# Order of the two transforms in a couple of ticks, and which banks they use

## The chip, the cores and the metric

The kernel runs on one core of a Trainium2 chip. The metric is the device time of one execution in microseconds; the figure for a kernel is the median of its runs. Engines are named as the profile names them: PE (TensorE matmuls), PEld (TensorE weight loads), DVE (VectorE), ACT (ScalarE), POOL (GpSimd) and SP (SyncE, which here only issues DMAs).

## The reference

`x` is (8, 5696, 128), eight batches. First a causal convolution along the sequence with the filter `h`, written as a product of spectra of the doubled length; then a spectral mix of the lowest 64 modes of that result, and a residual with one dense layer:

```python
Yf = rfft(x, n=2*S, axis=1) * rfft(h, n=2*S, axis=0)[None]
a  = irfft(Yf, n=2*S, axis=1)[:, :S]                  # (8, 5696, 128)
X  = rfft(a, axis=1)[:, :64]                          # 64 modes, complex
Y  = X times (w_r + i w_i), one 128x128 matrix per mode
u  = a + irfft(Y, n=S, axis=1)
out = u + relu(u @ w_ch)
```

## The kernel before

The sequence is cut as 5696 = 89 x 64, and every Fourier transform is made of matmuls with constant matrices in fp16. The batches go two at a time: four passes, `g_` = 0 to 3. A pass has a first transform (`a_tile`, 32 of them: a slice of `Xin` times `F1`, evacuated to `As`), then 26 ticks. In a tick `t` below 23, up to four of the 90 values of `k` are worked on, and four kinds of work follow one another:

- `second(g_, t)`, the second transform: 16 matmuls of `M` and `As` (64 rows in use, 128 columns), two accumulated per value of `k` and batch, into a slot of two PSUM banks, one per batch. The profile shows them as `ps<-As,M`. Sixteen is one tick, thirty-two is two ticks one behind the other.
- `products(g_, t, slot)`, the product with the filter's spectrum `Hs` on DVE, into one of three buffers `U` (L651). As a rule ACT first copies the slot from PSUM to a small fp16 buffer `Xs` (`copied`, one of two buffers), and DVE multiplies from there. In a tick called *straight* (`t % 4 == 3` in the passes after the first) there is no copy: DVE reads the slot in PSUM itself (the rows `U<-ps,Hs` of 2048 columns).
- With a lag of two ticks, `ps<-U,Wc`: four matmuls of 512 columns that turn `U` back along one axis, two per batch, into one of three PSUM banks (`ZBANK`) in turn. ACT evacuates each to `Zs` or `Zt`, and SP writes that to memory.
- With a lag of three ticks, `ps<-G,Zs`: sixteen short matmuls that gather the 64 modes in a bank of their own.

Each engine works through its own list in order; a recorder (`R.add`) follows which instruction reads and writes what, and adds semaphore waits between engines.

In the passes after the first, `twin(g_, t)` is true for odd `t`: the second transforms of `t` and `t + 1` are then issued together, and tick `t + 1` issues none. I call the two ticks a couple: (1,2), (3,4), ... (21,22). Those that start with a straight tick are (3,4), (7,8), (11,12), (15,16) and (19,20): five in a pass, fifteen in the three passes. In them the second tick is copied by ACT as a rule is.

The slot is one of `XSLOT = [0, 2]`, that is banks 0 and 1, or banks 2 and 3. A second transform that writes a slot must wait until ACT's copy, or DVE's straight product, has read what stood there.

In the same ticks DVE also places the next pass's input (`x_place`, L365, eight copies `Xin<-Xt` per pass), which POOL loads (`x_load`, two DMAs each, `Xt<-in_x_dram`, issued in tick `t` once the product of tick `t` is done). The last of the eight is loaded in tick 16 and placed at the top of tick 22; the next pass's first transform waits for all of them. A pass ends with the first transforms of the next one. After the fourth pass come the mix of the modes and the output stage (`u_tile`, `o_tile`).

Of the kernel before, what the change touches and what calls it, by code (L numbers as in the profile page):

```python
# [123 lines left out]
def bass_long_conv_fft__then__afno_spectral_mix_kernel(nc, x, h, moe_w_r, moe_w_i, moe_w_ch, out):  # L124
# [160 lines left out]
    def ap(t, row, p0, n, off, dims):  # L285
        return bass.AP(t, p0 * row + off, [[row, n]] + [list(d) for d in dims])
# [5 lines left out]
    def pv(bank, off, dims, p0=0, n=P):  # L292
        return bass.AP(ps, p0 * 4096 + bank * 512 + off, [[4096, n]] + [list(d) for d in dims])
# [5 lines left out]
    def bank(i):  # L299
        return ("bank", i)  # L300
# [3 lines left out]
    def evac(dst, src, reads, writes, scale=None, eng=None, after=()):  # L304
        e = eng
        if e is None:
            turn[0] ^= 1
            e = "scalar" if turn[0] else "vector"
        if e == "scalar":
            if scale is None:  # L310
                R.add(e, lambda h_: h_.copy(dst, src), reads, writes, after=after)  # L311
            else:
                R.add(e, lambda h_: h_.activation(dst, src, COPY, scale=scale), reads, writes, after=after)  # L313
        elif scale is None:
            R.add(e, lambda h_: h_.tensor_copy(dst, src), reads, writes, after=after)  # L315
        else:
            R.add(e, lambda h_: h_.tensor_scalar_mul(dst, src, scale), reads, writes, after=after)  # L317
# [4 lines left out]
    def mm(o, l, r, st, sp, reads, writes):  # L322
        R.add("tensor", lambda h_: h_.matmul(o, l, r, start=st, stop=sp), reads, writes)  # L323
# [11 lines left out]
    def turns(name, items):  # L335
        i = ring2.get(name, 0)
        ring2[name] = i + 1
        return items[i % len(items)]
# [25 lines left out]
    def x_place(i, src, toks):  # L364
        R.add("vector", lambda e: e.tensor_copy(bass.AP(x_sb, i * XN * XS, [[XW, NQ], [XS, XN], [1, D]]),  # L365
                                                src),
              list(toks) + XZ, [("xin", i)])
# [51 lines left out]
    def mtok(k):  # L419
        t = [("m", k // KP)]  # L420
        if k % KP == KP - 1 and k < NK - 1:
            t.append(("m", k // KP + 1))
        return t

    W1, W2, WI = wc_sb[:, 0:P], wc_sb[:, P:2 * P], wi_sb[:, :]
    XSLOT = [0, 2]
# [14 lines left out]
    for j in range(16):  # L441
        t = turns("h", [0, 2, 4])
# [36 lines left out]
    def xtok(n):  # L479
        return [("xt", n, p_) for p_ in range(2)]  # L480

    def x_room(g_, i):
        if g_ > 1:
            return x_st[i]
        return x_h[i] if i < NXH else x_st[i - NXH]
# [97 lines left out]
    def with_h_at(g_, t):  # L583
        return g_ == 0 and t + LH < NT
# [3 lines left out]
    def copied(g_, t, sl):  # L588
        n = len(ticks[t])
        e = onchip[(g_, t)] = turns("e", list(range(NXS)))  # L590
        evac(bass.AP(x_s[e], 0, [[1024, P], [512, 2], [1, n * D]]), pv(sl, 0, [[512, 2], [1, n * D]]), [bank(sl), bank(sl + 1)],
             [("xs", e)], eng="scalar")
        return e

    def twin(g_, t):
        return g_ > 0 and t % 2 == 1

    def straight(g_, t):
        return g_ > 0 and t % 4 == 3

    def slot_of(g_, t):
        if t == 0:
            return ZSLOT
        if g_ == 0:
            return XSLOT[(t + 1) % 2 if not with_h_at(g_, t) else 0]
        return XSLOT[((t - 1) // 4 + t) % 2]

    def second(g_, t, d0=0, d1=D, bs=(0, 1)):
        sl = slot_of(g_, t)
        rd = AST if d1 == D else [("as", j) for j in range(d1 // 4)]  # L610
        for i, k in enumerate(ticks[t]):
            for r in range(2):
                for b in bs:
                    col = k * 3 * J + (J if r == 0 else 0) + b * J
                    mm(pv(sl + b, i * D + d0, [[1, d1 - d0]]),
                       ap(m_sb, MW, J * b, J, col, [[1, P]]),
                       ap(a_sb, AW, J * b, J, (2 * k + r) * D + d0, [[1, d1 - d0]]), r == 0, r == 1,
                       rd + mtok(k), [bank(sl + b)])

    def first_u(b, s_, row, tok, d0, d1):  # L620
        n = len(ticks[0])
        R.add("vector", lambda e: e.tensor_tensor(  # L622
            bass.AP(u_s[0], b * 512 + d0, [[2048, P], [1024, 2], [D, n], [1, d1 - d0]]),
            bass.AP(s_[0], s_[1] + d0, [[row, P], [0, 2], [D, n], [1, d1 - d0]]),
            bass.AP(h_sb, d0, [[2 * HW, P], [HW, 2], [D, n], [1, d1 - d0]]), MULT),
              [tok, ("h", 0, 0), ("h", 0, 1, 0), ("h", 0, 1, J)], [("u", 0)])
# [36 lines left out]
    def tick(g_, t):  # L663
        if g_ + 1 < NP:
            for i in range(2 * XC):
                if t == XPLACE[g_ > 0][i]:
                    x_place(i, bass.AP(x_room(g_ + 1, i), 0, [[XB, NQ], [D, XN], [1, D]]), xtok(i))
        with_h = with_h_at(g_, t)
        if t < NT:
            of_two = t > 0 and twin(g_, t - 1)  # L670
            if not of_two:
                if t:
                    second(g_, t)
                if t == 1:
                    d_ = DA if g_ else DF
                    second(g_, 0, d_, D, (0,))
                    first_u(0, (ps, slot_of(g_, 0) * 512), 4096, bank(slot_of(g_, 0)), d_, D)
            products(g_, t, slot_of(g_, t))
            if twin(g_, t):
                second(g_, t + 1)  # L680
                if straight(g_, t):
                    copied(g_, t + 1, slot_of(g_, t + 1))
        drain = list(border[t]) if t in border and g_ + 1 < NP else []
        if drain and t >= NT:
            j, sl, e = drain.pop(0)
            a_tile(j, [sl], e)
        if g_ + 1 < NP:
            i = t // 2 - 1 if t % 2 == 0 else -1
            if g_ == 0:
                i = XLATE.index(t) + NXH if t in XLATE else -1  # L690
            if 0 <= i < 2 * XC:
                x_load(g_ + 1, i, x_room(g_ + 1, i), xtok(i), [("u", t % NU)] + AST)
        if LC <= t < NT + LC:
            s_ = t - LC
            n = len(ticks[s_])
            i, zi = s_ % NU, zroom(g_, s_)
            zb = [turns("z", ZBANK) for b in range(2)]
            for b in range(2):
                for r in range(2):
                    mm(pv(zb[b], 0, [[1, n * D]]), (W1, W2)[r], u_s[i][:, r * 1024 + b * 512:r * 1024 + b * 512 + n * D],  # L700
                       r == 0, r == 1, [("u", i), ("wc",)], [bank(zb[b])])
                evac(bass.AP(z_s[zi], b * D, [[1024, P], [2 * D, n], [1, D]]),
                     pv(zb[b], 0, [[D, n], [1, D]]), [bank(zb[b])], [("zs", zi, b)], eng="scalar",
                     after=once(("zx", zi, b), Z_OLD) if zi >= NZ else ())
            zo = (g_ * NK + KT * s_) * P * 256
            dma("sync", bass.AP(zs, zo, [[256, P], [P * 256, n], [1, 256]]),
                bass.AP(z_s[zi], 0, [[1024, P], [256, n], [1, 256]]), "z",
                [("zs", zi, 0), ("zs", zi, 1)], [("zd", g_, s_)])
            if drain and t >= NT:
                j, sl, e = drain.pop(0)  # L710
                a_tile(j, [sl], e)
        if LM <= t < NT + LM:
            s_ = t - LM
            zi = zroom(g_, s_)
            for i, k in sorted(enumerate(ticks[s_]), key=lambda q: (s_ > 0 or q[1] != 1, q)):
                for b in range(2):
                    if k % 2:
                        o, off, n, sl = pv(MB, b * P, [[1, P]]), (k + 1) // 2 * P, P, (k + 1) // 2
                    else:
                        ms, off = even[k]  # L720
                        n, sl = 2 * len(ms), 0
                        dims = [[M, 2]] if len(ms) == 1 else [[ms[1] - ms[0], 2], [M, 2]]
                        o = pv(MB, b * P + ms[0], dims)
                    mm(o, z_s[zi][:, i * 256 + b * P:i * 256 + b * P + P], g_sb[:, off:off + n],
                       k == 1 and b == 0, k == NK - 1 and b == 1, [("g", sl // GP), ("zs", zi, b)], [bank(MB)])
        if drain and t < NT + LM - 1:
            j, sl, e = drain.pop(0)
            a_tile(j, [sl], e)
        if with_h:
            filter_tick(t + LH, [2, 3])  # L730
# [230 lines left out]
```

## Time and profile before

| | |
|---|---|
| median of 3 runs | 378.37 us (377.17, 378.37, 379.49) |
| profiled execution, its own time | 377.96 us |
| its span on the core | 376.1 us |
| granted TensorE clock, mean | 0.992 |
| first pass, with the filter's own transform between its ticks | about 46 to 96 us |
| ticks of the second, third and fourth pass | about 108 to 143, 162 to 198, 217 to 255 us |
| mix and output stage | from about 256 us to the end |

The profile is one execution. Times in it are microseconds from the span's start. A row of its timeline gives the start, the time until the end of the last instruction merged into the row, the engine, the line, the operation, the output and the inputs, the shape, and the count; a bracket tells how long the engine sat idle before it, and what released it. On ACT and DVE the recorded end of an instruction lies somewhat behind the start of the next one, so the pace of an engine is read from start to start. All matmuls are issued from one helper line (L323), all plain ACT copies from another (L311), so groups go by the tiles' names.

### The profile page before, as it was taken

The numbers are of one execution on the slowest core, as the hardware profiler recorded it, in microseconds if no ns is written. First come the engines' busy times: TensorE is split into PE (matmuls) and PEld (weight loads), VectorE is DVE, ScalarE is ACT, GpSimd is POOL, SyncE is SP. The second block draws the span as 40 slices with busy tenths as digits, with TensorE's granted clock in tenths as the row PEclk, the third lists the DMA queues.
The fourth block names the chain that finished last, engine by engine and source line by source line (L and its number), as shares of the span: only waits on it lengthen the run. The fifth ranks groups of instructions, "written<-read, shape, count | busy, mean of one in ns | idle before, by whom it ended". The sixth has DMA issues, their size and how long they took to land.

```text
span 376.1 us, 12494 instructions
## 1 busy us (share of the span) xinstructions
PE 357.8 (95%) x5370; PEld 278.1 (74%) x5370; DVE 294.3 (78%) x335; ACT 315.7 (84%) x497; POOL 75.0 (20%) x117
## 2 busy tenths in 40 slices
PE   7979999999999999999998999999999999999994
PEld 7978866666866666856666856668889988888873
DVE  3548889978998999989998988883447767756666
ACT  8458899998999997989997999996557677688885
POOL 8703011200643220742310301124000000000000
PEclk9998999999999999999999999999999999999998
DMA  7999979979799997999995989999999999999878
GB/s 145 206 283 367 244 178 252 210 212 269 85 154 198 251 247 214 96 145 214 257 256 163 99 301 365 372 356 378 358 410 399 417 410 409 410 405 379 316 303 324
DMA packets 87048, 103.94 MB, mean 276 GB/s; under 512 B 22730, under 2 KB 72522, under 8 KB 83438
## 3 DMA queue, kind: packets, MB, share of 16 engines
q1 hardware_dynamic: 64610, 81.33, 61.1%
q0 software_dynamic: 22384, 21.83, 35.4%
q8 instruction: 42, 0.69, 0.7%
q14 instruction: 12, 0.10, 0.1%
HBM read 70.61 MB, written 51.12 MB: 324 GB/s over the span
## 4 chain that ended last, share of the span: by engine, by line
PE 67%; ACT 11%; DMA 10%; DVE 5%; issue 3%; POOL 3%; SPq 0%; DVEq 0%; POOLq 0%
PE ps L323 67%; ACT As L313 7%; DMA Hs<-Hs 4%; DMA Xr<-in_x_dram 4%; DVE As L317 2%; DMA Xt<-in_x_dram 2%; POOL Xr L320 2%; ACT Zs L311 1%; ACT R L893 1%; POOL Hin L320 1%; DVE Xin L365 1%; ACT Xs L311 1%; DVE U L622 1%; DVE Hs L315 1%; ACT Zt L311 1%
## 5 line engine op out<-in xcount | busy, mean ns | idle before, releaser
L651 DVE TENSOR_TENSOR U<-Xs,Hs 128x2048 f16<-128x2048 f16 (+1 forms) x73 | 86.6, 1192 | 13.9 <-ACT Xs L311 11.4
L323 PE MATMUL ps<-U,Wc 128*128 128x512 f16 (+1 forms) x368 | 94.1, 376 | 1.4 <-DVE U L622 1.4
L311 ACT CAST Xs<-ps 128x1024 f16<-128x1024 f32 (+1 forms) x77 | 74.7, 978 | 7.3 <-PE ps L323 4.2
L311 ACT CAST Zs<-ps 128x512 f16<-128x512 f32 (+1 forms) x132 | 69.2, 595 | 1.9 <-PE ps L323 1.9
L894 DVE TENSOR_TENSOR O<-ps,R 128x512 f32<-128x512 f32 x81 | 52.3, 684 | 20.7 <-ACT R L893 11.8
L317 DVE TENSOR_SCALAR As<-ps 128x720 f16<-128x720 f32 (+1 forms) x67 | 55.8, 881 | 6.7 <-PE ps L323 5.2
L893 ACT ACTIVATE R<-ps 128x512 f32<-128x512 f32 (+1 forms) x92 | 50.5, 592 | 9.0 <-PE ps L323 8.9
L323 PE MATMUL ps<-F,Xin 128*128 128x180 f16 x512 | 53.5, 254 | 4.4 <-DVE Xin L365 2.9
L323 PEld LDWEIGHTS ps<-F,Xin 128*128 128x128 f16 x512 | 45.8, 155 | 11.7 <-DVE As L317 3.3
L323 PE MATMUL ps<-As,M 64*128 64x128 f16 (+3 forms) x1504 | 52.3, 214 | 2.1 <-ACT As L313 1.3
L313 ACT ACTIVATE As<-ps 128x720 f16<-128x720 f32 (+1 forms) x65 | 46.2, 769 | 8.4 <-PE ps L323 7.8
L323 PE MATMUL ps<-WI,UT 128*128 128x256 f16 x360 | 51.0, 278 | 0.5 <-ACT UT L311 0.4
L323 PEld LDWEIGHTS ps<-U,Wc 128*128 128x128 f16 x368 | 28.7, 97 | 30.3 <-ACT Zs L311 3.7
L311 ACT CAST UT<-ps 128x712 f16<-128x712 f32 x46 | 34.5, 752 | 17.8 <-PE ps L323 16.8
L323 PEld LDWEIGHTS ps<-As,M 64*128 64x128 f16 x1504 | 42.2, 94 | 8.5 <-ACT As L313 1.8
L323 PEld LDWEIGHTS ps<-WI,UT 128*128 128x128 f16 x360 | 39.0, 152 | 3.4 <-issue 1.8
L323 PE MATMUL ps<-IBs,C 128*128 128x356 f16 x128 | 39.2, 314 | 0.2
L320 POOL DMA_DIRECT2D Xt<-in_x_dram x40 | 21.5, 541 | 78.7 <-PE ps L323 78.2
L323 PEld LDWEIGHTS ps<-G,Zs 128*128 128x128 f16 x512 | 26.1, 96 | 14.5 <-ACT Zs L311 2.0
L651 DVE TENSOR_TENSOR U<-ps,Hs 128x2048 f16<-128x2048 f32 x15 | 34.2, 2283 | 0.0
L323 PE MATMUL ps<-G,Zs 128*128 128x128 f16 (+2 forms) x512 | 32.2, 192 | 0.1
L311 ACT CAST Zt<-ps 128x512 f16<-128x512 f32 x52 | 28.5, 622 | 0.4 <-PE ps L323 0.4
(74 smaller groups left out, 480.0 us busy)
## 6 DMA issues: line engine op xcount, KB each, us to landing
out_dram<-O SPq DMA_DIRECT2D x39, 512.0 KB, 8.7
zscr<-Zs SPq DMA_DIRECT2D x62, 256.0 KB, 6.1
zscr<-Zt SPq DMA_DIRECT2D x26, 256.0 KB, 6.3
Xt<-in_x_dram POOLq DMA_DIRECT2D x20, 320.0 KB, 6.9
W<-wscr SPq DMA_DIRECT2D x4, 1024.0 KB, 7.2
ZT0a<-zscr SPq DMA_DIRECT2D x4, 1024.0 KB, 9.9
M<-cM POOLq DMA_DIRECT2D x5, 720.0 KB, 17.6
ZT1a<-zscr SPq DMA_DIRECT2D x3, 1024.0 KB, 10.6
```

Source lines behind the costliest of these rows:

```text
L311: R.add(e, lambda h_: h_.copy(dst, src), reads, writes, after=after)
L313: R.add(e, lambda h_: h_.activation(dst, src, COPY, scale=scale), reads, writes, after=after)
L315: R.add(e, lambda h_: h_.tensor_copy(dst, src), reads, writes, after=after)
L317: R.add(e, lambda h_: h_.tensor_scalar_mul(dst, src, scale), reads, writes, after=after)
L320: R.add(eng, lambda h_: h_.dma_start(dst, src), reads, writes, ring=ring, after=after)
L323: R.add("tensor", lambda h_: h_.matmul(o, l, r, start=st, stop=sp), reads, writes)
L365: R.add("vector", lambda e: e.tensor_copy(bass.AP(x_sb, i * XN * XS, [[XW, NQ], [XS, XN], [1, D]]), src), list(toks) + XZ, [("xin", i)])
L622: R.add("vector", lambda e: e.tensor_tensor(bass.AP(u_s[0], b * 512 + d0, [[2048, P], [1024, 2], [D, n], [1, d1 - d0]]), bass.AP(s_[0], s_ ...
L651: R.add("vector", lambda e: e.tensor_tensor(uv, src, hv, MULT), bk + [("h", t, 0), ("h", t, 1, 0), ("h", t, 1, J)], [("u", i)])
L893: R.add("scalar", lambda e: e.activation(rv, src_r, RELU), bk, [("r", i % NR)], after=once(("r", i % NR), G_ALL + XTT + [("y", 0), ("y", 1 ...
L894: R.add("vector", lambda e: e.tensor_tensor(ov, src_u, rv, ADD), bk + [("r", i % NR)], [key + (h_,)], after=once(key, old))
```

## The change

In a couple that starts with a straight tick, the second transform of `t + 1` is issued ahead of that of `t`. DVE's straight product and ACT's copy of `t + 1` are issued in the same places as before. The slots go by `t % 4`: ticks with remainder 0 and 1 take banks 0 and 1, those with 2 and 3 take banks 2 and 3.

```diff
     def slot_of(g_, t):
...
-        return XSLOT[((t - 1) // 4 + t) % 2]
+        return XSLOT[t % 4 // 2]
...
         if t < NT:
             of_two = t > 0 and twin(g_, t - 1)
             if not of_two:
+                if straight(g_, t):
+                    second(g_, t + 1)
                 if t:
                     second(g_, t)
...
             products(g_, t, slot_of(g_, t))
-            if twin(g_, t):
+            if straight(g_, t):
+                copied(g_, t + 1, slot_of(g_, t + 1))
+            elif twin(g_, t):
                 second(g_, t + 1)
-                if straight(g_, t):
-                    copied(g_, t + 1, slot_of(g_, t + 1))
```

In the order in which PE writes them, the slots before were, from tick 1 on, 2, 0, 2, 0 for ticks 1 to 4, then 0, 2, 0, 2 for 5 to 8, and so on by turns; now they are 0, 2, and then always 0, 2 again, where the copied tick of a straight couple comes first and takes banks 0 and 1, and the straight tick takes banks 2 and 3. So the lists of all five engines keep their length and their sequence of kinds. What differs in the waits is this: in each of the fifteen straight couples ACT's copy waits for a matmul 16 places earlier in PE's list than before, and DVE's straight product for one 16 places later.

## Prediction

> **What bounds the kernel now.** I read the page first, then the windows of the passes that the change touches, then the chain of waits, and last the timeline of one straight couple on PE, ACT and DVE. The page says that PE is at work almost all the time, and that the chain that ended last runs mostly through it:
>
> ```profile
> span 376.1 us, 12494 instructions
> PE 357.8 (95%) x5370; PEld 278.1 (74%) x5370; DVE 294.3 (78%) x335; ACT 315.7 (84%) x497; POOL 75.0 (20%) x117
> PE 67%; ACT 11%; DMA 10%; DVE 5%; issue 3%; POOL 3%; SPq 0%; DVEq 0%; POOLq 0%
> ```
>
> The windows give, for a stretch, its length and then the busy time of PE, PEld, DVE, ACT and POOL, the granted clock, the DMA share and GB/s. The first row is the ticks of the third pass, the second those of the fourth, the third a part of the output stage. Under them is a piece of the chain (start, length, engine):
>
> ```profile
> 162.50:198.00 35.50, 35.46 (x548) 22.61 (x549) 33.69 (x28) 34.42 (x56) 8.74 (x16) 1.00 1.06 224
> 217.30:252.00 34.70, 34.64 (x544) 22.18 (x545) 28.92 (x21) 33.63 (x54) 5.37 (x3) 1.00 1.02 347
> 263.00:314.00 51.00, 50.90 (x777) 45.39 (x774) 32.63 (x47) 33.64 (x56) 0.00 (x0) 1.00 1.01 399
> 162.54 27.27 PE ps L323 x430
> ```
>
> PE is the pace: 35.46 of 35.50 us, at full clock, and the chain stays on it for 27.27 us. ACT and DVE are close behind (34.42 and 33.69). So a matmul moved within PE's list is worth nothing by itself. The change can pay only through a wait inside PE's dense stretch, and a recorded matmul hides a short one. I look for it by comparing a straight couple with a plain one. Ticks 7 and 8 of the third pass are the couple at 170.55, ticks 9 and 10 the one at 174.11:
>
> ```profile
> 170.55 1.07 PE L323 MATMUL ps<-As,M 64*128 64x128 f16 x32
> 171.55 1.04 PE L323 MATMUL ps<-U,Wc 128*128 128x512 f16 x4
> 172.75 1.07 PE L323 MATMUL ps<-U,Wc 128*128 128x512 f16 x4
> 173.66 0.52 PE L323 MATMUL ps<-G,Zs 128*128 128x2 f16 x8
> 174.11 1.07 PE L323 MATMUL ps<-As,M 64*128 64x128 f16 x32
> 175.11 1.04 PE L323 MATMUL ps<-U,Wc 128*128 128x512 f16 x4
> 176.31 1.02 PE L323 MATMUL ps<-U,Wc 128*128 128x512 f16 x4
> 177.18 0.49 PE L323 MATMUL ps<-G,Zt 128*128 128x2 f16 x8
> 177.59 1.07 PE L323 MATMUL ps<-As,M 64*128 64x128 f16 x32
> ```
>
> The work is the same. The straight couple takes 174.11 - 170.55 = 3.56 us, the plain one 177.59 - 174.11 = 3.48. The 0.08 lies in two places: the second group of `U,Wc` (1.07 against 1.02) and the short matmuls behind it (0.52 against 0.49). Who holds them is seen on ACT and on PEld:
>
> ```profile
> 171.06 0.63 ACT L311 CAST Zs<-ps 128x512 f16<-128x512 f32 x1
> 171.66 1.01 ACT L311 CAST Xs<-ps 128x1024 f16<-128x1024 f32 x1
> 172.57 0.59 ACT L311 CAST Zs<-ps 128x512 f16<-128x512 f32 x1
> 172.57 1.08 ACT L311 CAST Zs<-ps 128x512 f16<-128x512 f32 x2
> 173.22 0.11 PEld L323 LDWEIGHTS ps<-U,Wc 128*128 128x128 f16 x2 [0.36 <-ACT Zs L311]
> 175.76 1.07 ACT L311 CAST Zt<-ps 128x512 f16<-128x512 f32 x2
> 176.72 1.03 ACT L311 CAST Xs<-ps 128x1024 f16<-128x1024 f32 x1
> ```
>
> There are three banks for the results of `U,Wc`. The third matmul at 172.75 (the second batch) writes the bank that ACT's evacuation at 172.57 empties. That one ends at 172.57 + 0.59 = 173.16, and the weight load goes at 173.22, released by it. The second evacuation of that pair ends at 172.57 + 1.08 = 173.65, when the short matmuls that read it begin (173.66). So in a straight couple PE runs into ACT, by 0.08 us.
>
> And ACT was late because of the copy in front: two evacuations take 176.72 - 175.76 = 0.96 from start to start, 0.48 each. ACT could have begun the copy at 171.06 + 0.48 = 171.54, but it began at 171.66, as the 32 matmuls ended (170.55 + 1.07 = 171.62). It waited 0.12 us for the second half of the couple.
>
> **The change part by part.**
>
> *ACT's copy.* In the changed order the copied tick is complete after the first 16 matmuls, half of 1.07: about 170.55 + 0.54 = 171.09. ACT is ready only at 171.54, so the copy starts there, 0.12 earlier. The two evacuations behind it move with it, since their matmuls (171.55 to 172.59) leave them room: 173.16 becomes 173.04, and with the 0.06 from there to the weight load 173.10. Without a stall, the third matmul is due at 172.75 + 2 x 0.217 = 173.18 (four of them take 177.18 - 176.31 = 0.87 from start to start in the plain couple). The bank is free in time by 0.08. The short matmuls, due 0.05 earlier at 173.61, find their data at 173.53. Both stalls go: 0.08 per straight couple, five a pass. PE is then late next on itself, at 3.48 per couple as in plain ones; ACT had 35.50 - 34.42 = 1.08 idle in the window of a pass, and keeps it.
>
> *DVE's straight product.* It now waits for all 32 matmuls, half a couple (0.54) more. DVE's rows, of ticks 6 and 7, and then of ticks 1 to 3 of the second pass with ACT's copy beside them:
>
> ```profile
> 170.81 1.23 DVE L651 TENSOR_TENSOR U<-Xs,Hs 128x2048 f16<-128x2048 f16 x1 [0.73 <-ACT Xs L311]
> 171.95 2.28 DVE L651 TENSOR_TENSOR U<-ps,Hs 128x2048 f16<-128x2048 f32 x1
> 107.82 2.35 DVE L651 TENSOR_TENSOR U<-Xs,Hs 128x2048 f16<-128x2048 f16 x2
> 110.09 2.28 DVE L651 TENSOR_TENSOR U<-ps,Hs 128x2048 f16<-128x2048 f32 x1
> 110.04 1.01 ACT L311 CAST Xs<-ps 128x1024 f16<-128x1024 f32 x1 [0.36 <-PE ps L323]
> ```
>
> Before the straight product DVE is busy with the product in front of it, so it comes at 171.95, when the couple has been complete since 171.62: 0.33 to spare, and the longer wait costs nothing. In the first straight couple of a pass the margin is small. There the copy, which in the old order waits for the same 32 matmuls, goes at 110.04, and the product at 110.09: 0.05 to spare. The Trainium skill, "Perfetto Trace Analysis", section "Tensor Engine Instruction (MATMUL, LD_WEIGHTS)", says that a matmul's end in a profile is estimated from its size and not observed. By that rule the 0.33 could be wrong, while the start of the copy at 110.04 stands, being an observed start on ACT; the trace agrees in that the copies start 0.04 behind the modelled ends (171.66 against 171.62). So I take this part at 0, between 0 and a delay of 0.54.
>
> *Slots.* Each write of a slot follows the reader of two transforms earlier, as before: the first of a straight couple follows a copy, the second a copy, and in the next couple the first follows the copy and the second the straight product. The straight product ends at 171.95 + 2.28 = 174.23; the transform that overwrites its slot is the second half of the couple at 174.11, that is 174.65. It has 0.42 to spare, 0.34 when PE comes 0.08 earlier. Ticks 1 and 2 swap slots behind the first transforms, but tick 1 waits for all of those in either order. I take 0.
>
> *What arrives at the end of a pass.* The gain must pass the placing of the next input, where PE waits:
>
> ```profile
> 144.31 0.85 PE L323 MATMUL ps<-F,Xin 128*128 128x180 f16 x8 [0.33 <-DVE Xin L365]
> 199.10 0.85 PE L323 MATMUL ps<-F,Xin 128*128 128x180 f16 x8 [0.54 <-DVE Xin L365]
> 138.49 2.28 DVE L651 TENSOR_TENSOR U<-ps,Hs 128x2048 f16<-128x2048 f32 x1
> 140.69 0.68 DVE L365 COPY Xin<-Xt 89x2048 f16<-89x2048 f16 x1
> 141.28 2.36 DVE L651 TENSOR_TENSOR U<-Xs,Hs 128x2048 f16<-128x2048 f16 x2
> 143.57 0.68 DVE L365 COPY Xin<-Xt 89x2048 f16<-89x2048 f16 x1
> 188.23 1.22 DVE L651 TENSOR_TENSOR U<-Xs,Hs 128x2048 f16<-128x2048 f16 x1
> 190.98 7.35 DMA Xt<-in_x_dram
> 198.35 0.69 DVE L365 COPY Xin<-Xt 89x2048 f16<-89x2048 f16 x1
> 190.98 0.93 POOL L320 DMA_DIRECT2D Xt<-in_x_dram  x1 [0.48 <-issue]
> 191.11 0.68 DVE L365 COPY Xin<-Xt 89x2048 f16<-89x2048 f16 x1
> 135.39 1.04 POOL L320 DMA_DIRECT2D Xt<-in_x_dram  x2 [2.29 <-PE ps L323]
> ```
>
> In the second pass DVE runs without a break from the straight product of tick 19 (138.49) to the last `Xin` (143.57). So the gains of the four earlier straight couples arrive, 4 x 0.08 = 0.32. In the third pass the last `Xin` at 198.35 waits for its load, which took 7.35 us from 190.98 (198.33). That load is issued behind the product of tick 16 (188.23), so it moves with the three couples before: 3 x 0.08 = 0.24. In the fourth pass no input is placed: 5 x 0.08 = 0.40. The output stage is PE's own (50.90 of 51.00) and moves as a whole. The sum is 0.32 + 0.24 + 0.40 = 0.96 us.
>
> A rule of the Trainium skill bears on the third pass: "SBUF — State Buffer", section "Who interferes with whom", says that a DVE copy can take the port pair shared with GpSimd for its whole length and so hold up the writing of DMA descriptors. The rows agree: the issue at 190.98 that met the copy at 191.11 took 0.93, where two in the second pass took 1.04 together. By that rule the term would be 0.24 if the copy and the issue still meet, as I expect since both hang on the same products, and up to 0.41 more (0.93 less half of 1.04) if they don't.
>
> **The sum.** The profiled execution took 377.96 us, 1.86 more than its span; less 0.96 it is 377.00. It lies 0.41 below the median of the three runs, so for a median I say 378.37 - 0.96 = 377.4.
>
> **The rivals.**
>
> *Nothing arrives* (378.4). The 0.08 is a matter of how matmuls are recorded, or the next load and the next placing take it back. For it: DVE has only 35.50 - 33.69 = 1.81 idle in a pass, and PE waits for DVE at two of the three pass ends. Against it: the weight load names its releaser, and the fourth pass has no such end.
>
> *ACT is the pace, not PE* (375.5). Then every wait taken from ACT counts in full: 0.12 in twelve couples and, in the first of each pass, the bracketed 0.36 and the 0.11 by which a recorded pair (1.07) exceeds its 0.96: 12 x 0.12 + 3 x 0.47 = 2.85. Against it: ACT's idle 1.08, and the chain, which is on PE.
>
> *The load at the pass's end comes later* (378.9). If the placing copies meet the second issue in the second pass too, it comes 0.48 + 0.41 = 0.89 later, as in the third; there the landing then sets the end in both, and 0.89 takes the place of 0.32 and 0.24: 378.37 + 0.89 - 0.40 = 378.9. It decides where an `Xin` copy begins before the issue has ended. Against it: both follow the same DVE products.
>
> *DVE waits for the transform* (up to 386). If the straight product began a whole half-couple later, and DVE, with its 1.81 idle, could not make it up: 15 x 0.54 = 8.1. It decides from the point where DVE is done more than 0.33 us before the couple is (0.05 in the first). The rows are all on the other side of it.
>
> **How the numbers follow.** The forecast gets 0.62, nothing 0.20, ACT as the pace 0.05, the later load 0.09, DVE waiting 0.04. Three runs of the same kernel span 2.3 us, so a median of few runs can lie 0.8 off. That takes the forecast from 376.4 to 378.4, nothing up to 379.3, the later load to 379.7. Together with most of the ACT case (375.5 and up), 375.8 to 379.6 holds 8 in 10. One per cent, 3.8 us, is about what a measurement of this kernel tells from no change. Below 374.6 lies only the far side of the ACT case, 0.04 with what I overlook; above 382.2 only DVE waiting with the same, 0.05; within, 0.91.
>
> **What would show it.** Right: straight couples at 3.48 on PE, their second `U,Wc` groups at 1.02, the weight load's bracket gone; ACT's copy 0.1 to 0.5 earlier behind the evacuation before it; straight products still back to back with the product before. Wrong: a bracket ahead of `U<-ps,Hs`, straight couples still at 3.56, or a longer bracket at the two rows `F,Xin`.

## The result, and the profile after

| | changed | before, same chip | ratio (95% interval) |
|---|---|---|---|
| the result, 22 runs each | 376.34 us | 377.53 us | 0.9969 (0.9955 to 0.9984) |
| run again (`r0_changed_again`) | 376.86 us | 377.33 us | 0.998 (0.9961 to 1.0) |
| run a third time (`r1_changed_third`) | 376.85 us | 377.24 us | 0.9983 (0.9967 to 0.9999) |

The change makes the kernel faster by 0.2 to 0.3% by the ratios (which are not simply the quotients of the medians beside them), and by 1.19, 0.47 and 0.39 us by the medians; the second interval reaches 1.0. The forecast was 0.96 us less than before, and 377.4 us; it counted from the first three runs of the kernel before, whose median of 378.37 lay 0.84 above that of 22. So 376.34 lies just below the 376.4 to 378.4 that the prediction gave its forecast, and within its wider range.

This is the couple of ticks 7 and 8 in the third pass of the changed kernel, from its timeline: PE's groups and the begin of the next couples, the weight load of the third matmul in the second group of `U,Wc`, then ACT, then DVE. The short matmuls are eight a tick, sixteen a couple.

```profile
169.78 1.07 PE L323 MATMUL ps<-As,M 64*128 64x128 f16 x32
170.78 1.04 PE L323 MATMUL ps<-U,Wc 128*128 128x512 f16 x4
171.65 0.49 PE L323 MATMUL ps<-G,Zs 128*128 128x2 f16 x8
171.98 1.02 PE L323 MATMUL ps<-U,Wc 128*128 128x512 f16 x4
172.84 0.49 PE L323 MATMUL ps<-G,Zs 128*128 128x2 f16 x8
173.27 1.07 PE L323 MATMUL ps<-As,M 64*128 64x128 f16 x32
176.74 1.07 PE L323 MATMUL ps<-As,M 64*128 64x128 f16 x32
...
172.37 0.14 PEld L323 LDWEIGHTS ps<-U,Wc 128*128 128x128 f16 x2 [0.29 <-ACT Zs L311]
...
169.80 1.11 ACT L311 CAST Zs<-ps 128x512 f16<-128x512 f32 x2
170.76 1.07 ACT L311 CAST Xs<-ps 128x1024 f16<-128x1024 f32 x1
171.66 0.65 ACT L311 CAST Zs<-ps 128x512 f16<-128x512 f32 x1
...
170.03 1.23 DVE L651 TENSOR_TENSOR U<-Xs,Hs 128x2048 f16<-128x2048 f16 x1 [0.73 <-ACT Xs L311]
171.17 2.28 DVE L651 TENSOR_TENSOR U<-ps,Hs 128x2048 f16<-128x2048 f32 x1
```

The straight couple takes 173.27 - 169.78 = 3.49 us where it took 3.56, the plain one behind it 176.74 - 173.27 = 3.47. The second group of `U,Wc` is down from 1.07 to 1.02, the short matmuls from 0.52 to 0.49. The weight load still waits for ACT, but it now goes at 172.37, and the third matmul, due at 171.98 + 2 x 0.217 = 172.41, no longer waits. ACT's copy begins 170.76 - 169.80 = 0.96 behind the start of the two evacuations, which is ACT's own pace, where it was 171.66 - 170.58 = 1.08. The row of the two evacuations in the kernel before:

```profile
170.58 1.11 ACT L311 CAST Zs<-ps 128x512 f16<-128x512 f32 x2
```

DVE's straight product has no bracket: it begins 1.39 after the couple, as before (171.95 - 170.55 = 1.40).

That profile is of the slowest of the 22 runs, at 379.94 us. Behind the passes PE waits for a load of the output stage, which the profile before does not show. First a row of PE's waits (the sum, how often, the longest), then the piece of the chain:

```profile
PE ps L323 <- DMA ZT2b<-zscr: 1.0, 1, 1.0
```

```profile
259.88 11.49 DMA ZT2b<-zscr
```

In the two later traces of the changed kernel (the last two rows of the table above) no wait of PE for ZT2b is listed. In the table below the traces are compared pass by pass. A pass is measured on PE from its first second transform to the first matmul of what follows it (`F,Xin` of the next pass, in the fourth pass `S4a,ZT0a`):

| pass | before | changed, with the result | again | third time | gain predicted |
|---|---|---|---|---|---|
| second | 104.86 to 144.31 = 39.45 | 39.16 | 39.17 | 39.18 | 0.32 |
| third | 159.40 to 199.10 = 39.70 | 39.59 | 39.24 | 39.17 | 0.24 |
| fourth | 214.21 to 255.90 = 41.69 | 41.39 | 41.30 | 41.30 | 0.40 |
| gain in all | | 0.70 | 1.13 | 1.19 | 0.96 |

### The profile page after: what moved, and what is told of

The parts are those of the page before. It is cut to its first block, busy times and chain, and to the rows that moved or that the text cites. A ratio compares the mean times of both kernels' runs of the same rounds, so it can differ in the third digit from the quotient of the medians.

```text
span 378.1 us, 12494 instructions
## 1 busy us (share of the span) xinstructions
PE 355.7 (94%) x5370; PEld 276.7 (73%) x5370; DVE 294.3 (78%) x335; ACT 315.0 (83%) x497; POOL 74.6 (20%) x117
## 4 chain that ended last, share of the span: by engine, by line
PE 61%; DMA 15%; ACT 10%; DVE 6%; POOL 3%; issue 3%; SPq 0%; DVEq 0%; POOLq 0%
PE ps L323 61%; ACT As L313 7%; DMA Xt<-in_x_dram 4%; DMA out_dram<-O 4%; DMA Xr<-in_x_dram 4%; DMA ZT2b<-zscr 3%; DVE As L317 3%; POOL Xr L320 2%; DVE U L651 1%; ACT R L895 1%; POOL Hin L320 1%; DVE Xin L365 1%; ACT Zs L311 1%; DVE U L622 1%; ACT Xs L311 1%
## 5 line engine op out<-in xcount | busy, mean ns | idle before, releaser
L311 ACT CAST Zs<-ps 128x512 f16<-128x512 f32 (+1 forms) x132 | 70.0, 600 | 2.6 <-PE ps L323 2.3
L323 PE MATMUL ps<-F,Xin 128*128 128x180 f16 x512 | 52.3, 250 | 3.5 <-DVE Xin L365 2.1
L323 PEld LDWEIGHTS ps<-F,Xin 128*128 128x128 f16 x512 | 44.5, 155 | 10.8 <-DVE As L317 3.0
```

## The experiments

**The two halves of the change by themselves.** The slots alone, transforms in the old order:

```diff
-        return XSLOT[((t - 1) // 4 + t) % 2]
+        return XSLOT[t % 4 // 2]
```

> The kernel before with the slots by t mod 4 alone, the transforms in the old order. Theory: the straight tick's transform now overwrites the slot that the tick before it used, whose copy ends at about 170.70 in the profile before, while PE would begin at 170.55; PE stalls about 0.2 us at the start of 12 straight couples (not in the first of a pass, whose copy is long done), and ACT's copy still waits for the second half. 12 x 0.2, some of it lost at the pass ends: 1.8 to 2.4 us slower than before, ratio 1.005 to 1.0065. Rival (the banks by themselves bring the gain): ratio 0.997.

Measured: 379.43 us, ratio 1.0051 (1.0033 to 1.0068). The other half is the changed kernel with that line put back.

> The changed kernel with the old slots, that is the new order of the transforms alone. Theory: the copied tick's transform comes first and overwrites the slot that ACT has just been copying, so PE stalls 0.2 us at the start of 12 straight couples; ACT's copy is then still ready in time (171.3 against 171.54), so the 0.08 is gained in each of 15. Net about 0.12 a couple: 0.5 to 1.5 us slower than before, ratio 1.0015 to 1.004. Rival (the order alone brings the gain, the slots are ballast): ratio 0.997.

Measured: 378.25 us, ratio 1.002 (1.0001 to 1.0039). The timeline of the slots alone, PE about ticks 7 and 8 and the copy of tick 6 on ACT:

```profile
170.44 0.49 PE L323 MATMUL ps<-G,Zs 128*128 128x2 f16 x8
171.07 1.07 PE L323 MATMUL ps<-As,M 64*128 64x128 f16 x32
174.63 1.07 PE L323 MATMUL ps<-As,M 64*128 64x128 f16 x32
...
169.98 1.03 ACT L311 CAST Xs<-ps 128x1024 f16<-128x1024 f32 x1
```

The couple begins 0.63 behind the short matmuls, where 0.41 to 0.45 is usual: PE waits for the copy, which ends at 169.98 + 1.03 = 171.01. And it still takes 174.63 - 171.07 = 3.56. For the order alone, the same rows:

```profile
166.54 1.07 PE L323 MATMUL ps<-As,M 64*128 64x128 f16 x32
170.23 1.07 PE L323 MATMUL ps<-As,M 64*128 64x128 f16 x32
173.71 0.51 PE L323 MATMUL ps<-As,M 64*128 64x128 f16 x12
...
169.14 1.03 ACT L311 CAST Xs<-ps 128x1024 f16<-128x1024 f32 x1
```

The plain couple in front takes 170.23 - 166.54 = 3.69, which is 0.21 more, for the same reason; but the straight couple takes 3.48. So the order takes the 0.08 away, and the slots keep it from costing 0.21. Neither half is faster by itself: the banks are no gain, they make room for the order.

**The same wait taken away in another way.** The kernel before, in its old order and with its old slots; in straight couples ACT's copy leaves out the last 64 columns of each bank, so the product of these columns is taken with older values.

```diff
-        evac(bass.AP(x_s[e], 0, [[1024, P], [512, 2], [1, n * D]]), pv(sl, 0, [[512, 2], [1, n * D]]), ...
+        w = n * D - (64 if straight(g_, t - 1) else 0)
+        evac(bass.AP(x_s[e], 0, [[1024, P], [512, 2], [1, w]]), pv(sl, 0, [[512, 2], [1, w]]), ...
```

> The kernel before, old order and slots, with ACT's copy in straight couples 64 columns shorter in each of the two banks (896 instead of 1024; the columns left out keep what the buffer held). Theory: the copy starts as late as before but ends about 0.11 us sooner, so the two evacuations behind it come 0.11 sooner, and PE's waits go as with the change: straight couples at 3.48 to 3.50 us, ratio 0.996 to 0.9985. Rival (the order of the transforms or the banks matter in another way than through ACT): straight couples stay at 3.56, ratio 1.000.

Measured: 376.52 us, ratio 0.9972 (0.9953 to 0.999). PE and ACT about ticks 7 and 8:

```profile
169.74 1.07 PE L323 MATMUL ps<-As,M 64*128 64x128 f16 x32
173.22 0.96 PE L323 MATMUL ps<-As,M 64*128 64x128 f16 x28
...
170.84 0.91 ACT L311 CAST Xs<-ps 128x896 f16<-128x896 f32 x1
171.65 1.08 ACT L311 CAST Zs<-ps 128x512 f16<-128x512 f32 x2
```

The copy still begins late, 1.10 after the couple (1.11 before the change), but gives way after 0.81 us in place of 0.91. The couple takes 3.48. The order of the transforms is not needed for the gain; what counts is when ACT gets to the evacuations.

**The wait put back.** The changed kernel with ACT's copy in straight couples as four instructions of 256 columns:

```diff
+        parts = [(i, q) for i in range(2) for q in range(2)] if straight(g_, t - 1) else [(0, 0)]
+        if len(parts) > 1:
+            for i, q in parts:
+                evac(bass.AP(x_s[e], i * 512 + q * 256, [[1024, P], [1, 256]]), pv(sl + i, q * 256, [[1, 256]]), ...
+            return e
```

> The changed kernel with ACT's copy in straight couples cut into four instructions of 256 columns, so that ACT is longer at it. Estimate from rows: an evacuation of 512 columns takes 0.48 from start to start and a copy of 1024 takes 0.91, so about 0.05 is fixed per instruction and three more cost about 0.15 us. Theory: the evacuations behind it come 0.15 later than in the changed kernel, 0.03 later than before the change; PE's waits return in full, straight couples at 3.56 to 3.60 us, ratio to before 0.999 to 1.002. Rival (ACT does not set it): couples stay at 3.49, ratio 0.997.

Measured: 378.6 us, ratio 1.0027 (1.0011 to 1.0043). The sign is the theory's, the size is not. PE, PEld and ACT about ticks 7 and 8:

```profile
170.02 1.07 PE L323 MATMUL ps<-As,M 64*128 64x128 f16 x32
172.22 1.19 PE L323 MATMUL ps<-U,Wc 128*128 128x512 f16 x4
173.69 1.07 PE L323 MATMUL ps<-As,M 64*128 64x128 f16 x32
...
172.80 0.10 PEld L323 LDWEIGHTS ps<-U,Wc 128*128 128x128 f16 x1 [0.48 <-ACT Zs L311]
...
171.00 1.26 ACT L311 CAST Xs<-ps 128x256 f16<-128x256 f32 x4
172.06 0.69 ACT L311 CAST Zs<-ps 128x512 f16<-128x512 f32 x1
```

The couple takes 3.67, twelve of them 3.67 or 3.68; the first of each pass stays at 3.48, where the copy had a bracket of 0.36 to give. The copy costs 172.06 - 171.00 = 1.06, which is 0.16 more than the 0.90 of the changed kernel, as estimated. The evacuation behind it begins 2.04 after the couple, close to the 2.02 before the change; yet PE loses 0.20 and not 0.1. The reason is in its own row: it takes 0.69 us to its end, where the one before the change took 0.59, so the bank is free 0.12 later (last section).

**What limits the passes now.**

> The changed kernel once more, for a second profile: the one taken with the result held a wait of about 1 us for a ZT2b load at the start of the output stage, and took 379.94 us. Theory (ACT's copy no longer waits for the second half of a straight couple, so PE's two short waits behind it go): straight couples at 3.48 to 3.49 us on PE in all three passes, ratio to before 0.996 to 0.9985, no such load wait. Rival (the gain is elsewhere, or the wait for the ZT load belongs to the change): the load wait is there again, and the time gained does not match 15 x 0.08 us less what the pass ends take.

Measured: the ratio of the table above; straight couples at 3.48 or 3.49 in all three passes, no wait for a ZT load by DMA. Then three versions for the end of a pass. The first issues the next input's loads a tick earlier:

```diff
-            i = t // 2 - 1 if t % 2 == 0 else -1
+            i = t // 2 if t % 2 == 1 else -1
```

> The changed kernel with the loads of the next input issued one tick earlier in the second and third pass (odd ticks 1 to 15 in place of even ticks 2 to 16). Theory: the end of the third pass hangs on the landing of the last load (7.35 us), that of the second on DVE's own row; with the load 1.7 us earlier the third pass becomes like the second: 0.2 to 0.5 us less than the changed kernel, ratio to before 0.995 to 0.9975. Rival (the landing does not set the pass's end): the same as the changed kernel.

Measured: 376.2 us, ratio 0.9977 (0.9956 to 0.9998). The third pass takes 39.14, against 39.24 and 39.17 in the later traces of the changed kernel without it, so nothing can be told apart. In the latter (`r1_changed_third`) the last placing waits for DVE and not for its load; in the former (`r0_changed_again`) the load lands at 196.81 and the placing begins at 196.83, only 0.07 after DVE was ready for it, so there was little left to gain. The next version has the early loads too, and the last placing one tick earlier (`XPLACE` ends in 20, 21 in place of 20, 22):

> The one before it, and the last placing of the next input at the top of tick 21 instead of tick 22, ahead of that tick's product on DVE. Theory: PE's idle time ahead of the first transform at the pass ends (0.33 and 0.54 us before) goes, and the gains of the last straight couple arrive too: 0.5 to 1.1 us less than the changed kernel, ratio to before 0.994 to 0.9965. Rival (the delayed product of tick 21 is then late for the matmuls of tick 23, or the load is late for tick 21): no gain over the changed kernel, PE waits for DVE's product instead.

Measured: 376.68 us, ratio 0.9978 (0.996 to 0.9996). Second and third pass take 38.60 us each, 0.57 and 0.64 less than in `r0_changed_again`. But from there to the next pass's second transforms it takes 15.52 in place of 15.09. DVE's rows at the end of the second pass, first of the changed kernel run again, then of this one:

```profile
140.24 2.35 DVE L651 TENSOR_TENSOR U<-Xs,Hs 128x2048 f16<-128x2048 f16 x2
142.50 0.68 DVE L365 COPY Xin<-Xt 89x2048 f16<-89x2048 f16 x1
143.11 0.68 DVE L651 TENSOR_TENSOR U<-Xs,Hs 128x1024 f16<-128x1024 f16 x1
143.83 2.54 DVE L317 TENSOR_SCALAR As<-ps 128x720 f16<-128x720 f32 x3
```

```profile
140.42 1.21 DVE L651 TENSOR_TENSOR U<-Xs,Hs 128x2048 f16<-128x2048 f16 x1
141.55 0.68 DVE L365 COPY Xin<-Xt 89x2048 f16<-89x2048 f16 x1
142.15 1.82 DVE L651 TENSOR_TENSOR U<-Xs,Hs 128x2048 f16<-128x2048 f16 x2
143.89 2.53 DVE L317 TENSOR_SCALAR As<-ps 128x720 f16<-128x720 f32 x3
```

The same work stands ahead of the first evacuation to `As`, only in another order. Counted from the pass's first second transform, that evacuation comes 0.14 sooner (143.89 - 104.28 = 39.61 against 143.83 - 104.08 = 39.75), which is what is left of the 0.57 after 0.43 was given back. PE starts earlier and then waits for DVE. So the last version takes a placing out of DVE's tail and puts it where DVE sat idle for 0.73 ahead of the product of tick 6. The loads are issued at odd ticks and no longer wait for the tick's product, which gives them the time.

```diff
-    XPLACE = ..., [9, 10, 13, 14, 17, 18, 20, 22]
+    XPLACE = ..., [6, 9, 10, 13, 14, 17, 18, 20]
...
-            i = t // 2 - 1 if t % 2 == 0 else -1
+            i = t // 2 if t % 2 == 1 else -1
...
-                x_load(g_ + 1, i, x_room(g_ + 1, i), xtok(i), [("u", t % NU)] + AST)
+                x_load(g_ + 1, i, x_room(g_ + 1, i), xtok(i), ([] if g_ else [("u", t % NU)]) + AST)
```

> The changed kernel with the loads of the next input at odd ticks, waiting for the second transforms alone (not for the tick's product), and with the eight placings at ticks 6, 9, 10, 13, 14, 17, 18, 20 in place of 9, 10, 13, 14, 17, 18, 20, 22. The run that only moved the last placing ahead of a product gained 0.57 and 0.64 us up to the first transform of the next pass and gave 0.43 back in each behind it, since DVE still had all of it to do before the first As evacuation (143.89 against 143.83). Theory (at a pass's end DVE is what is late next, so only work taken out of its tail counts): one placing of 0.6 us goes into DVE's idle time of 0.7 ahead of the product of tick 6; the first As evacuation of the two following passes comes about 0.5 us sooner: 0.6 to 1.2 us less than the changed kernel, ratio to before 0.9935 to 0.996. Rival (the first placing, or the one at tick 20, meets a load that has not landed, and DVE stalls in the couples): straight or plain couples over 3.55 us, no gain over the changed kernel.

> The changed kernel beside it on the same chip, to compare the two directly. Both theories: ratio to before 0.996 to 0.9985, straight couples at 3.49 us.

Measured together on one chip: 375.38 us against 376.85, ratios to before 0.9947 (0.9921 to 0.9973) and 0.9983 (0.9967 to 0.9999). DVE's rows at tick 6 of the second pass and at its end:

```profile
113.60 1.23 DVE L651 TENSOR_TENSOR U<-Xs,Hs 128x2048 f16<-128x2048 f16 x1 [0.68 <-ACT Xs L311]
114.74 0.68 DVE L365 COPY Xin<-Xt 89x2048 f16<-89x2048 f16 x1
115.56 1.23 DVE L651 TENSOR_TENSOR U<-Xs,Hs 128x2048 f16<-128x2048 f16 x1
...
140.17 0.68 DVE L365 COPY Xin<-Xt 89x2048 f16<-89x2048 f16 x1
140.77 2.95 DVE L651 TENSOR_TENSOR U<-Xs,Hs 128x2048 f16<-128x2048 f16 x3
```

The placing fills the idle time before tick 6, and none stands between the last products. The couples stay at 3.48 and 3.49. From one pass's second transforms to the next's, the traces have 158.29 - 104.25 = 54.04 and 212.09 - 158.29 = 53.80 us, against 54.28 (158.63 - 104.35 and 212.91 - 158.63, both) in `r1_changed_third`: 0.72 in two passes. That is half of the 1.47 between the medians. Most of the rest of the difference between the two traces lies behind the passes, where the code is the same: from `S4a,ZT0a` to the end 373.08 - 253.40 = 119.68 us against 374.78 - 254.21 = 120.57, and traces differ there by as much anyway (119.53 in `e2`, 120.77 in `e1`). So the passes show 0.72; the intervals of the two ratios overlap, and that the rest comes of the version is not shown. By its median this is the fastest of the versions, and the only one whose interval lies wholly below 0.998.

## Why the prediction was right

*PE is the pace, and waits for ACT in straight couples.* Right. Taking the wait away by the order (`after`) or by a shorter copy (`e3`) brings couples to 3.48 to 3.49 and the time to 0.997; putting it back by a longer copy (`e4`) brings both back and more. The rival by which ACT is the pace is out: in the first couple of a pass ACT's wait of 0.36 went as well, and the couple gained 0.08 like the others (3.56 to 3.48). *Nothing arrives* is out by the interval of the result, which ends at 0.9984, and by the gain of 0.70 to 1.19 us in the passes of all three traces. How well the time fits is partly luck: the three medians put the gain anywhere from 0.39 to 1.19 us. The one per cent that the prediction took for the limit of a measurement was too wide; with 22 runs each the interval is 0.15% to either side.

*The copy 0.12 earlier, both stalls gone.* Right, with less to spare than worked out. The evacuation begins 1.88 after the couple (171.66 - 169.78) where it was 2.02, but takes 0.65 in place of 0.59. With the 0.06 to the weight load, the bank is free at 1.88 + 0.65 + 0.06 = 2.59; the third matmul is due at 173.18 - 170.55 = 2.63. That leaves 0.04 and not 0.08 (the rows have the weight load at 172.37 - 169.78 = 2.59).

*DVE's longer wait costs nothing.* Right, in the first couple of a pass too: in the third pass of the changed kernel the straight product follows the two products in front of it at 2.26, as it did at 2.27 (110.09 - 107.82). Below are these rows, and from the page of that profile the group of all fifteen straight products, where the last number is DVE's idle time before them.

```profile
161.71 2.35 DVE L651 TENSOR_TENSOR U<-Xs,Hs 128x2048 f16<-128x2048 f16 x2
163.97 2.28 DVE L651 TENSOR_TENSOR U<-ps,Hs 128x2048 f16<-128x2048 f32 x1
...
L651 DVE TENSOR_TENSOR U<-ps,Hs 128x2048 f16<-128x2048 f32 x15 | 34.2, 2283 | 0.0
```

The warning of the Trainium skill ("Perfetto Trace Analysis", "Tensor Engine Instruction (MATMUL, LD_WEIGHTS)") that a matmul's end is estimated would have mattered most in those three couples, where the margin is smallest, and there is no wait in the rows.

*Slots cost nothing.* Right in this order. `e1` and `e2` show what the pairing is worth: 0.21 in twelve couples, if a slot is overwritten by the very next transform.

*What arrives at the ends of the passes.* 0.32 and 0.40 were right to 0.05 in the second pass and, in two of three traces, to 0.01 in the fourth. The third pass was the term with the wrong size: 0.24, and measured 0.11, 0.46 and 0.53. The step itself held: counted from the pass's first second transform, the last transfer is issued 0.25 earlier in all three traces (190.98 - 159.40 = 31.58 before; 190.06 - 158.73, 189.67 - 158.34 and 189.96 - 158.63, each 31.33, after). But the term was sized by its landing in one profile, 7.35 us after the issue, and in the three traces it landed after 7.20, 7.14 and 6.95 us. In the trace with the smallest gain a transfer of the load before took longer still (8.45 us, in the two others 6.6), and the placing of tick 20 waited for it:

```profile
186.23 8.45 DMA Xt<-in_x_dram
194.70 0.69 DVE L365 COPY Xin<-Xt 89x2048 f16<-89x2048 f16 x1 [0.29 <-DMA Xt<-in_x_dram]
```

In the third trace the loads had landed, and the end was DVE's as in the second pass; in `r0_changed_again` the last load came 0.07 after DVE was ready. In these two the last issue met a placing and took 0.91 and 0.92, as it would by the rule of the Trainium skill on the port shared by DVE and GpSimd ("SBUF — State Buffer", "Who interferes with whom"). In the first trace the issue took 0.53 and the placing 0.77 in place of 0.68, and there the gain was the smallest. So that meeting does not decide; how long the transfers take does. Why transfers of the same size differ by over a microsecond was not tried. The rival of a later load in the second pass did not come about: its last two issues took 1.03 or 1.04 together, as before.

*Two of the signs named ahead did not come as named.* The weight load's bracket is not gone, it went from 0.36 to 0.29: the load still waits for ACT, and what went is PE's wait for it. And the bracket at `F,Xin` at the end of the second pass is longer, 0.38 in all three traces where it was 0.33. It was listed as a sign of being wrong, but the prediction's own sum lets the gain of the fifth couple end in that wait.

*Not foreseen.* The wait of 1 us and more for a ZT2b load behind the passes, in two of eleven traces (the changed kernel's first, and `e5`). In the former the stage from `S4a,ZT0a` to the end of the span takes 378.09 - 254.80 = 123.29 us, against 376.10 - 255.90 = 120.20 in the kernel before. PE's rows there:

```profile
265.41 0.20 PE L323 MATMUL ps<-S4b,ZT0b 84*128 84x89 f16 x1 [1.12 <-issue]
270.20 0.21 PE L323 MATMUL ps<-S4a,ZT2a 128*128 128x89 f16 x1 [0.42 <-DMA ZT2a<-zscr]
271.42 0.21 PE L323 MATMUL ps<-S4b,ZT2b 84*128 84x89 f16 x1 [1.00 <-DMA ZT2b<-zscr]
```

Matmul by matmul beside `r0_changed_again`, PE falls back by 1.3, 0.6 and 1.2 us at these three. So the two loads account for 1.8 of the 3 us; what held PE at the first place the profile does not name. In the two later traces of the changed kernel that stage takes 120.01 and 120.57, so it neither adds to the gain of the passes nor takes from it by more than such traces differ. Both kernels have single runs near 380 us (before 380.83 at most, changed 379.94), but no trace of such a run of the kernel before was taken. Whether it is the same wait stays open.

## What to carry to other kernels

Where the busiest engine shows no gaps, compare two stretches that do the same work: 3.56 against 3.48 told of a wait that no row of PE listed as idle. Then ask which engine holds the buffer, and what stands in front of that on its list; making that one item ready earlier is worth as much as making it shorter. An order that frees one wait can need the buffers dealt out anew, since the next writer of a buffer moves too.

## What the runs showed of the hardware

An evacuation on ACT ends later the more instructions ACT has run without a pause. Rows of single evacuations of 512 columns, the seventh in a row in the changed kernel run again and the thirteenth in `e4_copy_in_four`:

```profile
171.27 0.66 ACT L311 CAST Zs<-ps 128x512 f16<-128x512 f32 x1
```

```profile
173.49 0.73 ACT L311 CAST Zt<-ps 128x512 f16<-128x512 f32 x1
```

After a pause the first takes 0.585 us, the second 0.592, and each instruction behind them, whatever its size, adds 0.013: 0.605, 0.62 and so on, 0.73 for the thirteenth. The pace from start to start stays at 0.48, and a pause of 0.1 us starts the count anew. It is no matter of recording alone, for the waiting engine follows the end: in `e4` the evacuation ends at 172.06 + 0.69 = 172.75, and the weight load that waits for it goes at 172.80; in the changed kernel 171.66 + 0.65 = 172.31 and 172.37. The Trainium skill ("Perfetto Trace Analysis", section "Optimizing Scalar/DVE Operations") says that the acknowledgement of an instruction's writes overlaps with the next instruction; the rows agree, 0.59 to the end at a pace of 0.48. Whether it is the writes or their acknowledgement that falls behind in a long row, the rows do not tell. So an early start on a busy engine can buy less than it seems: the 0.14 by which the evacuation starts earlier (2.02 less 1.88) became 0.08 at its end.
